# The first product of experts 1 to 7 by one level of Strassen's method, all of it ahead of the second product

## The chip, the core and the metric

The kernel runs on one core of one Trainium2 chip. The metric is the device time of one launch in microseconds (us). The core has TensorE (PE, with its weight loads PEld), VectorE (DVE), ScalarE (ACT), GpSimd (POOL) and SyncE (SP), which here only issues transfers. Matmuls accumulate into PSUM, which has 8 banks of 128 x 512 numbers in single precision; all other tiles lie in SBUF, 128 partitions wide.

## The reference, cut to what matters

Attention over q, k, v (4 batches, 8 heads, 768 positions, 64 numbers a head; a window of 128 positions and 4 sink positions) gives 3072 rows x of 512 numbers. A gate picks two of eight experts for each row, with weights that sum to one. Then:

```python
out = np.zeros((N, D), dtype=np.float32)          # N = 3072, D = 512, F = 1024, E = 8
for e in range(E):
    for k in range(2):
        mask = top2[:, k] == e
        if not mask.any():
            continue
        h = np.maximum(x[mask] @ w1[e], 0.0)          # first product, 512 -> 1024
        out[mask] += top2_w[mask, k, None] * (h @ w2[e])   # second product, 1024 -> 512
```

## The kernel before, in words

**Arithmetic.** Inputs are single precision. Each factor is split in a high and a low part, and one block product is three matmuls: high weight by high x, high by low, low by high. Here ScalarE writes the high part and VectorE (a subtraction) the low part, for weights, rows and the hidden layer; some of expert 0's low parts are POOL's.

**Order.** A class `Plan` collects operations, each with an engine, an estimated cost, a priority and the tiles that it reads and writes. `Plan.run` simulates a list scheduler with those costs and then writes every operation out in the simulated order, so each engine's order is fixed when the program is built. Tiles stand in rings of two to nine buffers; a buffer's next use waits for the last reader of its previous use. A first plan holds the attention of all batches, the routing of the first three and the start of expert 0; a second plan holds the routing of the last batch, the rest of expert 0 and experts 1 to 7.

**Experts.** Experts 1 to 7 are sorted by load at run time; a table `who` holds their numbers (the loads of weights read it from a register) and `perm` picks a row's weight. Experts 0 to 7 in this order have room for 832, 832, 832, 800, 800, 768, 768, 768 rows: six tiles of 128 rows, and for the first five a seventh, narrow tile of 64 or 32. Each of experts 1 to 7 is worked in two pieces, tiles 0 to 2 (384 rows) and the rest (448, 416 or 384); expert 0 in pieces of 512 and 320 rows, the first of rows of the first three batches.

**A piece.** For each of 8 blocks of 128 hidden columns: the first product (`up`, 4 x 3 matmuls, L1070 to L1072, into one of two banks `H`), relu into the high part (`up_h`, ACT, L1081) and the low part (`up_l`, DVE, L1088) of a hidden tile `h` (ring of nine), then the second product of that block (`down`, L1099 to L1101, three matmuls for each full tile of rows into one of four banks `Y`; a narrow tile takes two, L1104 and L1105). So groups of 12 first-product matmuls alternate with 9 or 11 of the second product. The last piece alone does all its first products first and then its second products tile by tile. After the last block a tile is scaled by its weight into `y` (ACT, L1108; for a narrow tile L1111 on ACT and L1115, L1119 on DVE) and added to the output by an indirect DMA, which POOL issues (L1123, behind a memset of `spacer`, L1122; ring of four). The output is filled with zeros ahead of it (`out<-zt`, L1268, issued on SP).

**Rows.** The rows lie in a DRAM table `x_rows`, 4 parts of 128 numbers and 8 weights each. Expert 0 gathers whole rows (L897 on POOL, one indirect DMA a tile), and its tiles are transposed on PE (`TX`, L947). Experts 1 to 7 gather in quarters of 32 rows (L903, ring `xg` of five), each pair or triple of them behind a one-element copy on POOL that waits for a certain hidden block (`gate`, L1132). VectorE picks a row's weight (`gw`, `wc`, L1036, L1038) and transposes the tile in 32 x 32 blocks (L952, `xtn`); ACT writes the high part (L961, `skn`) and DVE the low part (L197, `sqn`). L197 is the line of a helper `minus` that all subtractions go through.

**Weights.** Each expert has four chunks of W1 (all 512 rows by 256 columns) and four of W2 (256 rows by 512), 512 KB each, through a staging ring `st` of two (L998 in four transfers a chunk, L1005 in one), ACT L1008 for the high part (`w`, `w2a`, `w2b`) and DVE L197 for the low part.

**Routing of the last batch.** It ends with matmuls on PE that place each row in its expert's list ("placing", L812) and spread the lists (L859); the late rows of expert 0 are gathered behind it.

Of the kernel before, what the change touches and what calls it, by code (L numbers as in the profile page):

```python
# [46 lines left out]
class Plan:  # L47
# [5 lines left out]
    def __init__(self, nc, pools, rings, cold=0.0):  # L53
# [8 lines left out]
        self.wrote = {}  # L62

    def get(self, tag, i, shape=None, dt=F32, pool="sb", pad=None):
        kx = (tag, i)
# [4 lines left out]

    def op(self, eng, dur, prio, fn, r=(), w=(), u=(), lat=None, kind=0):
# [4 lines left out]
        for kx in list(r) + list(w) + list(u):  # L76
# [88 lines left out]

class Shape:
# [33 lines left out]
def attention(tc, plan, consts, cst, sh, q, k, v, xbuf):  # L200
# [6 lines left out]
    plan.rings.update(vr=2, kn=2, qn=2, vn=2, dv=2, skn=2, sqn=2, kq=2, C=5, mn=3, sm=4, ri=2, pc=3,  # L207
# [323 lines left out]
def routing_setup(nc, pool, tmp, cst, sh, w_gate, w_noise, noise):  # L531
# [45 lines left out]
    c["quad"] = quad[1]  # L577
    c["most"] = pool.tile([128, 1], F32, name="most")
# [63 lines left out]
def routing(nc, plan, cst, sh, b, t0, nt, z, xbuf):  # L642
# [188 lines left out]
    if ends:  # L831
# [8 lines left out]
        if last:  # L840
# [9 lines left out]
            ordered(lambda: rt("idr", [128, E - 1, TE]), "idw")  # L850
        else:
            dve(lambda: v.tensor_tensor(tab("idx"), where()[:, fl], tab("sa"), op=OP.add), [("X", xi), ("sa", i)], [("idx", i)], .13)
    if last:
# [3 lines left out]
        def spread():  # L857
            for q in range(4):
# [31 lines left out]
def gather(plan, nc, cst, sh, xbuf, e, t, z, after=None):  # L890


    n = sh.TE * e + t
    first = not e and t < sh.FA

    def go():
        nc.gpsimd.indirect_dma_start(  # L897
            out=plan.get("xg", n, [128, sh.XW], F32, "early"), out_offset=None, in_=xbuf[:128 + sh.NA] if first else xbuf,
            in_offset=bass.IndirectOffsetOnAxis(ap=cst["idg"][:, t:t + 1], axis=0))

    def part(i):
        x = plan.get("xg", n, [128, sh.XW], F32, "early").rearrange("p (i d) -> p i d", d=sh.SW)
        nc.gpsimd.indirect_dma_start(  # L903
# [485 lines left out]
```

## Time and profile before

| | |
|---|---|
| runs | 806.75, 802.84, 803.80 us; median 803.8 |
| profiled execution, span | 802.8 us |
| matmuls on PE | 4753; busy 772.3 us (96%) |
| DVE, ACT, POOL busy | 54%, 43%, 55% |
| attention and routing, start of expert 0 | 0 to about 220 us |
| expert 0 with the last batch's routing | about 220 to 305 us |
| experts 1 to 7 | 305 to 795.2 us |
| last store | 795.2 to 802.8 us |

Rows of groups read: line, engine, operation, tiles (`out<-in`), partitions by columns, count; then busy time and mean ns of one; then the idle time of the engine just before them and what ended it. Rows of the timeline read: start in us, duration, engine, line, operation. Rows of a stretch read: from:to, length, busy time of PE, PEld, DVE, ACT and POOL with the number of instructions, the granted clock of TensorE (1 is full speed), the mean busy share of the 16 DMA engines and the GB/s. Rows of waits read: who waits, for whom, then total us, count and mean. Busy times of PE overlap, since matmuls are pipelined.

### The profile page before, as it was taken

The page shows a single profiled execution, that of the slowest core. Times are in us where ns is not written, and L with a number is a line of the kernel's source. Part 1 is how long each engine was busy: PE and PEld are TensorE (multiplying, and loading weights), DVE is VectorE, ACT ScalarE, POOL GpSimd, SP SyncE. Part 2 cuts the span into 40 slices and gives each one's busy share as a digit, 9 for nine tenths or more (in the row PEclk, how much of TensorE's full clock was granted, in tenths as well). Part 3 has the DMA queues.
Part 4 walks back from the last instruction along what each step waited for, and adds up shares of the span by engine and source line. Part 5 has one row for each costly group of instructions (what it writes and reads, how often), then busy time and mean ns, then how long its engine had stood idle before and what let it go on. Part 6 is the DMA issues. An engine that isn't in the chain of part 4 may idle for free.

```text
span 802.8 us, 13806 instructions
## 1 busy us (share of the span) xinstructions
PE 772.3 (96%) x4753; PEld 656.1 (82%) x4753; DVE 434.3 (54%) x1115; ACT 342.6 (43%) x695; POOL 441.5 (55%) x669
## 2 busy tenths in 40 slices
PE   7999999899798999999999999999999999999996
PEld 4776777677577888988988898899889999999994
DVE  5888897798565345354435434542553363364320
ACT  5877778686420334244233413332442343334121
POOL 5757657778604447473745456374636647366222
PEclk9999999999999999999999999999999999999998
DMA  6769767845526196264526535561744365174133
GB/s 121 169 150 200 162 155 207 181 120 129 152 90 175 22 257 152 45 140 128 102 38 158 141 56 94 144 119 37 147 123 94 73 172 121 26 175 97 32 40 40
DMA packets 151193, 96.03 MB, mean 120 GB/s; under 512 B 100528, under 2 KB 129200, under 8 KB 151120
## 3 DMA queue, kind: packets, MB, share of 16 engines
q1 hardware_dynamic: 137744, 67.93, 32.6%
q0 software_dynamic: 13376, 27.19, 19.4%
q8 instruction: 38, 0.62, 0.3%
q14 instruction: 35, 0.29, 0.1%
HBM read 66.89 MB, written 28.20 MB: 118 GB/s over the span
## 4 chain that ended last, share of the span: by engine, by line
PE 64%; issue 4%; DMA 2%; POOL 2%; DVE 1%; SPq 0%; ACT 0%; POOLq 0%; DVEq 0%; ACTq 0%
PE H L1070 11%; PE H L1072 10%; PE H L1071 10%; PE Y L1099 10%; PE Y L1101 10%; PE Y L1100 10%; POOL out L1123 1%; PE Y L1104 1%; PE Y L1105 1%; DMA xg<-x_rows,idg 1%; DMA out<-y,idx 1%; DMA st<-in_moe_w 1%; SPq L1268 0%; PE T L947 0%; PE X L616 0%
## 5 line engine op out<-in xcount | busy, mean ns | idle before, releaser
L903 POOL DMA_INDIRECT xg<-x_rows,rt_idq x174 | 175.8, 1010 | 62.1 <-issue 51.7
L1070 PE MATMUL H<-skn,w 128*128 128x384 f32 (+4 forms) x512 | 178.3, 348 | 0.0
L1072 PE MATMUL H<-skn,w 128*128 128x384 f32 (+4 forms) x512 | 176.8, 345 | 0.0
L1071 PE MATMUL H<-sqn,w 128*128 128x384 f32 (+4 forms) x512 | 176.3, 344 | 0.0
L1088 DVE SCALAR_TENSOR_TENSOR h<-H,h 128x384 fp32r<-128x384 f32 (+4 forms) x168 | 75.5, 469 | 184.7 <-ACT h L1081 184.5
L1081 ACT ACTIVATE h<-H 128x384 fp32r<-128x384 f32 (+4 forms) x128 | 64.6, 505 | 249.4 <-PE H L1072 249.3
L1132 POOL COPY spacer<-h 1x1 f32<-1x1 f32 x88 | 26.6, 303 | 167.3 <-ACT h L1081 167.1
L1123 POOL DMA_INDIRECT out<-y,idx x53 | 89.2, 1683 | 50.4 <-ACT y L1108 34.6
L1070 PEld LDWEIGHTS H<-skn,w 128*128 128x128 f32 x512 | 96.6, 189 | 7.7 <-issue 0.8
L1071 PEld LDWEIGHTS H<-sqn,w 128*128 128x128 f32 x512 | 96.6, 189 | 6.9
L1072 PEld LDWEIGHTS H<-skn,w 128*128 128x128 f32 x512 | 96.4, 188 | 3.0
L1101 PE MATMUL Y<-w2b,h 128*128 128x512 f32 x192 | 75.2, 392 | 1.1 <-DVE h L1088 1.1
L1099 PE MATMUL Y<-w2b,h 128*128 128x512 f32 x192 | 75.5, 393 | 0.6 <-ACT h L1081 0.6
L1099 PE MATMUL Y<-w2a,h 128*128 128x512 f32 x192 | 75.5, 393 | 0.0
L1100 PE MATMUL Y<-w2b,h 128*128 128x512 f32 x192 | 75.2, 392 | 0.0
L1100 PE MATMUL Y<-w2a,h 128*128 128x512 f32 x192 | 75.1, 391 | 0.0
L1101 PE MATMUL Y<-w2a,h 128*128 128x512 f32 x192 | 74.9, 390 | 0.0
L197 POOL TENSOR_TENSOR cbuf<-cbuf,mn 128x528 f32<-128x528 f32 x48 | 52.6, 1098 | 18.5 <-DVE mn L330 10.7
L310 PE MATMUL S<-kq 64*128 64x264 f32 (+1 forms) x384 | 56.4, 410 | 1.0 <-DVE ri L348 0.5
L961 ACT ACTIVATE skn<-xtn 128x512 fp32r<-128x512 f32 (+2 forms) x46 | 27.9, 606 | 63.3 <-DVE xtn L952 63.2
L197 DVE TENSOR_TENSOR w<-st,w 128x1024 fp32r<-128x1024 f32 x28 | 34.3, 1224 | 17.8 <-ACT w L1008 17.8
L1101 PEld LDWEIGHTS Y<-w2b,h 128*128 128x128 f32 x192 | 36.1, 188 | 9.4 <-DVE h L1088 1.6
(209 smaller groups left out, 1359.6 us busy)
## 6 DMA issues: line engine op xcount, KB each, us to landing
st<-in_moe_w SPq DMA_DIRECT2D x36, 512.0 KB
st<-in_moe_w SPq DMA_DIRECT2D x112, 128.0 KB
out<-zt SPq DMA_DIRECT2D x31, 256.0 KB
vn<-in_v SPq DMA_DIRECT2D x16, 384.0 KB
x_rows<-xr SPq DMA_DIRECT2D x48, 128.0 KB
kn<-in_k SPq DMA_DIRECT2D x30, 192.0 KB
qn<-in_q SPq DMA_DIRECT2D x30, 192.0 KB
xg<-x_rows,rt_idq POOLq DMA_INDIRECT x174, 2.9
```

Source lines behind the costliest of these rows:

```text
L197: eng.tensor_tensor(out, a, b, op=OP.subtract)
L310: nc.tensor.matmul(p[:, :2 if j else 1], kq(g)[r, j // 2, 2 + j % 2, NS:], x[:, :2 if j else 1], start=True, stop=True)
L903: nc.gpsimd.indirect_dma_start(out=x[:, i, :], out_offset=None, in_=xbuf.rearrange("r (q d) -> (r q) d", d=sh.SW), in_offset=bass.Indirect ...
L1070: nc.tensor.matmul(p, w[:, 0, i], xh, start=(i == 0), stop=False)
L1071: nc.tensor.matmul(p, w[:, 0, i], xl, start=False, stop=False)
L1072: nc.tensor.matmul(p, w[:, 1, i], xh, start=False, stop=(i == DC - 1))
L1081: nc.scalar.activation(get("h", FC * q + f, [128, 2 * 128 * FIRST], F32R)[:, :width], get("H", FC * q + f), AF.Relu)
L1088: nc.vector.scalar_tensor_tensor(h[:, o:o + s1 - s0], p[:, s0:s1], 0.0, h[:, s0:s1].bitcast(F32), op0=OP.max, op1=OP.subtract)
L1099: nc.tensor.matmul(p, hh, w[:, 0], start=(f == 0), stop=False)
L1100: nc.tensor.matmul(p, hh, w[:, 1], start=False, stop=False)
L1101: nc.tensor.matmul(p, hl, w[:, 0], start=False, stop=(f == FC - 1))
L1123: d = nc.gpsimd.indirect_dma_start(out=out, out_offset=bass.IndirectOffsetOnAxis(ap=c["idx"][:size(e, t), e, t:t + 1], axis=0), in_=get("y ...
```

## The change

Experts 1 to 7 do the first product by one level of Strassen's method in Winograd's form. W1 is halved in rows and in columns, and the expert's rows are halved (tiles 0, 1, 2 and half of the narrow tile against tiles 3, 4, 5 and the other half), so that x.W1 is a 2 x 2 block product. It takes 7 products of half size in place of 8: for each of 4 groups of 128 + 128 hidden columns 7 products of 6 matmuls over 416, 400 or 384 columns, 168 matmuls an expert in place of 192 (8 blocks of two pieces of 12); 1176 in place of 1344 for the seven experts. Three of the products take plain blocks of W1, four take sums of blocks; three take plain halves of x, four take sums. New work:

- POOL makes the four sums of each W1 chunk in place in `st` (L1083 one addition, L222 three subtractions, 128 x 256 each); ACT and DVE split the plain blocks and the sums (2 + 1 operations each).
- DVE transposes a pair of tiles into a raw tile `rw` (L1329), splits it, mixes its quarters (four subtractions), splits the result, into a fixed tile `XO`.
- Three banks a group: ACT copies three partial results to `ts` (L1394), DVE adds three others to them (`total`, L1400), then relu (ACT L1411) and the low part (DVE L1418), into one fixed hidden tile `hid` for all 8 blocks.
- All 28 products of an expert stand ahead of its second products (L1274 to L1276, narrow tile L1278 and L1279), whose tiles end staggered by up to two blocks (`SKEW`); tiles keep one bank for all 8 blocks. Expert 0 does its 8 first products ahead of its second ones too, in each piece.
- All 8 banks are fixed and shared by name (`B`, `H`, `Y`, `X`, `TX`); weights stand in one fixed tile `Z` with three slots for mixed W1 chunks (`W`, `Wd`) and three for W2 chunks (`V`); `xg` has four buffers, `st` two, `y` four.
- The gates are gone; gathers are issued up to four tiles ahead. Expert 1 gathers whole rows (seven DMAs with `idg1`), transposes on PE and loads each W1 chunk in one transfer; experts 2 to 7 keep the quarters. The planner counts 1.05 us for a quarter gather where it counted 1.25, 1.7 for a store as before, 0.72 for a sum on POOL.
- The zero fills hang on the blocks of expert 0's first piece, no longer on both pieces.

The diff, cut to its core (`mixed_x` and the aliases of the fixed buffers are told above):

```diff
 def gather(...):
-    for i in range(min(128, sh.CAPS[e] - 128 * t) // 32):
-        plan.op("Pool", 1.25, z + i, lambda i=i: part(i), r=[("rt_idq", sh.B - 1)] + (after(t, i) if after else []),
-                w=[("xg", n, i)], u=[("xg", n)], lat=3)
+    if e < 2:
+        plan.op("Pool", 1.25, z, row, r=[("idg1", 0) if e else ("idg", int(not early))], w=[("xg", n)], lat=3)
+        return n
+    for i in range(size // 32):
+        plan.op("Pool", 1.05, z + i, lambda i=i: part(i), r=[("idq", 0)], w=[("xg", n, i)], u=[("xg", n)], lat=3)
...
+def w_mixed(plan, nc, cst, sh, w1, e, i, z):
...
+    def mix(j):
+        _, a, b, c, d = raw()
+        if j == 0:
+            nc.gpsimd.tensor_tensor(d, c, d, op=OP.add)
+        else:
+            minus(nc.gpsimd, *((c, a, c), (a, d, a), (b, b, a))[j - 1])
...
+    plan.op("ACT", .6, z, lambda: direct_hi(0, 4), st, [kd])
+    plan.op("ACT", .37, z, lambda: direct_hi(4, 2), st, [kd])
+    plan.op("DVE", .69, z + .1, lambda: direct_lo(0, 4), st, [kd])
+    plan.op("DVE", .43, z + .1, lambda: direct_lo(4, 2), st, [kd])
+    for j in range(4):
+        plan.op("Pool", .72, z + .1, lambda j=j: mix(j), [], st)
+    plan.op("ACT", 1.04, z, mixed_hi, st, [kc])
+    plan.op("DVE", 1.22, z + .1, mixed_lo, st, [kc])
...
-    def up(q, f):
-        for i in range(DC):
-            xh, xl = (x[:, i, :width] for x in both)
-            nc.tensor.matmul(p, w[:, 0, i], xh, start=(i == 0), stop=False)
-            nc.tensor.matmul(p, w[:, 0, i], xl, start=False, stop=False)
-            nc.tensor.matmul(p, w[:, 1, i], xh, start=False, stop=(i == DC - 1))
...
+    MUL = {1: ("A11", 0, 0), 5: ("S1", 6, 1), 6: ("S2", 12, 0), 2: ("A12", 2, 2), 3: ("S4", 4, 1), 7: ("S3", 10, 0), 4: ("A22", 8, 0)}
...
+        def product(f, x):
+            u, o, b = MUL[x]
+            key = ("B", B[f][b])
+            fresh = x in (1, 5, 2)
...
+                for i in range(2):
+                    wh, wl = (mixed_block(c, k, u, y, i) for y in range(2))
+                    xh, xl = (XO()[:, y, o + i, :W] for y in range(2))
+                    nc.tensor.matmul(p, wh, xh, start=(fresh and i == 0), stop=False, skip_group_check=True)
+                    nc.tensor.matmul(p, wh, xl, start=False, stop=False, skip_group_check=True)
+                    nc.tensor.matmul(p, wl, xh, start=False, stop=(i == 1), skip_group_check=True)
...
+            seq += [(f, 1), (f, 5)] + ([(f - 1, 4)] if f else []) + [(f, 6), (f, 2), (f, 3), (f, 7)]
...
+    for e in range(1, E):
+        mixed_x(e, D[e - 1] + 1 if e > 1 else -80)
...
+                mix_w(e, i, D[e - 1] + 8 + 5 * i if e > 1 else 40 + 7 * i)
...
+        load_v(e, 0, U[e] - 3)
+        def rest(e=e):
+            mix_w(e, 3, U[e] + 6)
+            load_v(e, 1, U[e] + 12)
+            load_v(e, 2, U[e] + 18)
+        ups(e, U[e], ks[e], rest)
```

The order that this makes is shown at three places; numbers behind names are those of buffers. PE first, inside expert 1 before the change: `H` banks take first products, `Y` banks second ones.

```order
L1070 MATMUL H<-skn,w_5075 128x448
L1071 MATMUL H<-sqn,w_5075 128x448
L1072 MATMUL H<-skn,w_5075 128x448
L1099 MATMUL Y<-w2b,h 128x512
L1100 MATMUL Y<-w2b,h 128x512
L1101 MATMUL Y<-w2b,h 128x512
L1104 MATMUL Y<-w2b,h 128x512
L1105 MATMUL Y<-w2b,h 128x512
```

PE after the change, where expert 1's first products end and its second ones begin (`bank` is one of the eight banks):

```order
L1384 MATMUL bank_3594<-XO,Z 128x416
L1385 MATMUL bank_3594<-XO,Z 128x416
L1386 MATMUL bank_3594<-XO,Z 128x416
L1274 MATMUL bank_3597<-Z,hid 128x512
L1275 MATMUL bank_3597<-Z,hid 128x512
L1276 MATMUL bank_3597<-Z,hid 128x512
L1384 MATMUL bank_3591<-XO,Z 128x416
L1385 MATMUL bank_3591<-XO,Z 128x416
L1386 MATMUL bank_3591<-XO,Z 128x416
L1278 MATMUL bank_3590<-Z,hid 128x512
L1279 MATMUL bank_3590<-Z,hid 128x512
```

The two kinds of product alternated through the whole expert; now they mix at this seam alone, with the first second-product groups between the last two products. In the start of the second plan, PE now has 138 matmuls of expert 0 ahead of the placing matmuls where it had 108, and 21 between these and the transposes of expert 0's late rows in both.

POOL before, during a middle expert: quarter gathers in twos and threes behind gates, and stores of finished tiles between them.

```order
L903 DMA xg<-x_rows,rt_idq 128x136 x2
L1132 COPY spacer<-h 1x1
L903 DMA xg<-x_rows,rt_idq 128x136 x3
L1132 COPY spacer<-h 1x1
L903 DMA xg<-x_rows,rt_idq 128x136 x2
L1132 COPY spacer<-h 1x1
L903 DMA xg<-x_rows,rt_idq 128x136 x2
L1122 MEMSET spacer 1x1
L1123 DMA out<-y,idx 3968x512
```

POOL after, as the next expert's first chunk of W1 has been staged:

```order
L941 DMA xg_77<-x_rows,idqt 128x136
L1083 TENSOR_TENSOR st_72<-st_72 128x2x128
L941 DMA xg_74<-x_rows,idqt 128x136
L222 TENSOR_TENSOR st_72<-st_72 128x2x128
L941 DMA xg_74<-x_rows,idqt 128x136
L222 TENSOR_TENSOR st_72<-st_72 128x2x128
L941 DMA xg_74<-x_rows,idqt 128x136
L222 TENSOR_TENSOR st_72<-st_72 128x2x128
```

The gates left the queue, and the sums of W1 came in between the gathers of the next expert's rows.

DVE before, inside expert 1: low parts of hidden blocks (L1088) with weights and rows of the next piece between them.

```order
L1088 SCALAR_TENSOR_TENSOR h<-H,h 128x384
L1088 SCALAR_TENSOR_TENSOR h<-H,h 128x64
L197 TENSOR_TENSOR w_4910<-st,w_4910 128x1024
L1036 TENSOR_TENSOR gw<-xg,perm 32x8 x4
L1038 TENSOR_REDUCE wc_126<-gw 128x1
L952 STREAM_TRANSPOSE xtn<-xg 128x512
L1088 SCALAR_TENSOR_TENSOR h<-H,h 128x384
```

DVE after, near the end of expert 1's first products:

```order
L1400 TENSOR_TENSOR ts<-ts,bank_3597 128x416
L1400 TENSOR_TENSOR ts<-ts,bank_3594 128x416
L1329 STREAM_TRANSPOSE rw<-xg_75 128x4x4x32
L1418 SCALAR_TENSOR_TENSOR hid<-ts,hid 128x384
L1418 SCALAR_TENSOR_TENSOR hid<-ts,hid 128x32
L968 TENSOR_TENSOR gw_3602<-xg_75,permq 128x32
L970 TENSOR_REDUCE wc_138<-gw_3602 128x1
L1418 SCALAR_TENSOR_TENSOR hid<-bank_3597,hid 128x384
```

The totals (`ts`) and the hidden low parts stand in one queue with the transposes and weight rows (`gw`) of the next expert's gathered tiles.

More of the change, by code (lines that the diff above doesn't have):

```diff
@@ L887, in experts_setup, with gather, row @@
     c["wc"] = [pool.tile([128, sh.TE], F32, name=f"wc{i}") for i in range(2)]
[L890 to L896, printed above, removed]
+def gather(plan, nc, c, sh, xbuf, e, t, z):
+    n = plan.next("xg")
+    size = min(128, sh.CAPS[e] - 128 * t)
+    early = not e and t < sh.FA
+    def row():
+        idx = c["idg1"] if e else c["idg"]
         nc.gpsimd.indirect_dma_start(
-            out=plan.get("xg", n, [128, sh.XW], F32, "early"), out_offset=None, in_=xbuf[:128 + sh.NA] if first else xbuf,
-            in_offset=bass.IndirectOffsetOnAxis(ap=cst["idg"][:, t:t + 1], axis=0))
+            out=plan.get("xg", n, [128, sh.XW], F32, "early")[:size], out_offset=None, in_=xbuf[:128 + sh.NA] if early else xbuf,
+            in_offset=bass.IndirectOffsetOnAxis(ap=idx[:size, t:t + 1], axis=0))
@@ L1099, in down, with products @@
+    def products(p, f, w, hh, hl, both, r):
+        if both is None:
             nc.tensor.matmul(p, hh, w[:, 0], start=(f == 0), stop=False)
@@ new lines, in products, with XO, temp, raw @@
+            nc.tensor.matmul(p[:2 * r], both, w[:, 0], start=(f == 0), stop=False)
+            nc.tensor.matmul(p[:2 * r], both, w[:, 1], start=False, stop=(f == FC - 1))
+    def XO():
+        return get("XO", 0, [128, 2, 14, sh.CAP // 2], F32R, "late")
+    def temp(n):
+        return get("ts", 0, [128, 4, sh.CAP // 2], F32, "late")[:, n % 4]
+    def raw(n):
+        return get("rw", 0, [128, 2, 8, 128], F32, "late")[:, n % 2]
+    def pairs(e):
+        return [(0, 3), (1, 4), (2, 5)] + ([(TF,)] if R[e] else [])
@@ new lines, in experts, with alias @@
+    sh_xg = {e: {} for e in range(E)}
+    for t in range(FA, TE):
+        n = gather(plan, nc, c, sh, xbuf, 0, t, -110)
+        weight(plan, nc, c, sh, 0, t, n, -100)
+        rows_turn(plan, nc, c, sh, t, size(0, t), "TX", -100, n)
+    U, D = {}, {}
+    U[0], D[0] = 0.0, first(0, 0.0)
+    at = first(1, D[0])
+    for e in range(1, E):
+        U[e], D[e] = at, at + 168 * cost(sh.CAPS[e] // 2)
+        at = D[e] + FC * sum(.69 if t < TF else .46 for t in tiles_of(e))
+    def alias(k, *keys):
+        plan.behind[k] = keys
```

682 lines of the change are left out of this document (449 added, 233 removed).

## The prediction

> **What bounds the kernel now.** First the page's engine totals, then a split of the span at the places where the work changes character, then the waits of TensorE alone.
>
> ```profile
> span 802.8 us, 13806 instructions
> PE 772.3 (96%) x4753; PEld 656.1 (82%) x4753; DVE 434.3 (54%) x1115; ACT 342.6 (43%) x695; POOL 441.5 (55%) x669
> ...
> 0.00:220.00 220.00, 201.68 (x1902) 149.43 (x1902) 178.76 (x484) 155.53 (x401) 149.94 (x290) 0.99 0.68 159
> 220.00:305.00 85.00, 80.42 (x434) 65.96 (x431) 43.51 (x136) 23.74 (x40) 29.47 (x44) 0.98 0.50 135
> 305.00:795.20 490.20, 490.20 (x2423) 440.71 (x2421) 212.07 (x495) 162.66 (x253) 260.48 (x336) 1.00 0.46 101
> 795.20:802.80 7.60, 0.01 (x1) 0.00 (x0) 0.00 (x0) 0.69 (x1) 1.57 (x1) 0.66 0.29 36
> ...
> PE TX L947 <- DMA xg<-x_rows,idg: 2.7, 1, 2.7
> PE Y L1101 <- DVE h L1088: 1.1, 1, 1.1
> PE Y L1099 <- ACT h L1081: 0.6, 1, 0.6
> ```
>
> The stretches list length, then busy time of PE, PEld, DVE, ACT and POOL. From 305 to 795.2 us, experts 1 to 7, TensorE is busy 490.20 of 490.20 us, while DVE is at 43%, ACT at 33% and POOL at 53%. After 220 us TensorE waits three times, 4.4 us in all. So a microsecond of matmul taken out of that stretch is a microsecond of the end, as long as the three other engines, which have room, stay in time. The attention up to 220 us keeps its order; the tail of 7.6 us (last store) keeps its form. Both are costed at nothing.
>
> **The matmuls removed.** Busy times of matmuls overlap, so I price by the distance of starts. The first and the thirteenth start of groups of twelve, and of nine matmuls of the second product:
>
> ```profile
> 308.49 0.34 PE L1070 MATMUL H<-skn,w 128*128 128x384 f32 x1
> 310.60 0.40 PE L1099 MATMUL Y<-w2a,h 128*128 128x512 f32 x1
> ...
> 347.04 0.37 PE L1070 MATMUL H<-skn,w 128*128 128x448 f32 x1
> 349.49 0.39 PE L1099 MATMUL Y<-w2a,h 128*128 128x512 f32 x1
> ...
> 506.76 0.35 PE L1070 MATMUL H<-skn,w 128*128 128x416 f32 x1
> 509.04 0.39 PE L1099 MATMUL Y<-w2b,h 128*128 128x512 f32 x1
> ...
> 641.26 0.40 PE L1099 MATMUL Y<-w2a,h 128*128 128x512 f32 x1
> 643.32 0.34 PE L1070 MATMUL H<-skn,w 128*128 128x384 f32 x1
> ```
>
> Twelve take 2.11 us at 384 columns, 2.28 at 416, 2.45 at 448. Before, one expert has eight rounds of both pieces: 8 x (2.11 + 2.45) = 36.5 us for 832 rows, 8 x (2.11 + 2.28) = 35.1 for 800, 8 x 4.22 = 33.8 for 768; for two, two and three experts 244.5 us. After, each has 28 products of 6 matmuls over half the rows: 168 x 0.190 = 31.9 us (416 columns), 168 x 0.183 = 30.7 (400, midway between rows), 168 x 0.176 = 29.6 (384); together 214.0. **Term 1: -30.5 us.** The second product keeps its matmuls, 8 x 20 x 0.229 (2.06 us for nine) = 36.6 us for 832 or 800 rows, 33.0 for 768. Per expert TensorE then needs 68.5 us (832), 67.3 (800) and 62.6 (768).
>
> **Alternation.** Nine second-product matmuls between two first-product groups take 2.06 us. If the pairing costs 0.03 us each of 16 x 7 times, its removal gives 3 us; if nothing, 0. The new order still alternates near the seam. **Term 2: -2 us** (0 to -3).
>
> **Transposes of expert 1.** They move from VectorE's 32-blocks to TensorE, seven tiles; the row of such a tile and the start after it:
>
> ```profile
> 263.00 0.60 PE L947 MATMUL TX<-idf,xg 128*128 128x128 f32 x4
> 263.35 0.47 PE L1099 MATMUL Y<-w2b,h 128*128 128x512 f32 x1
> ```
>
> 7 x 0.35: **term 3: +2.5 us.** Expert 1's 26 quarter gathers become 7 row gathers on POOL, and its four weight loads issue once each instead of four times on SP: both are relief. The zero fills moved up in SP's queue, ahead of the loads of the experts' numbers, lie beside expert 0's 44 us of matmuls; if that cover failed, expert 1's first weights would be late by those issues, a delay that the bounds of term 4 hold.
>
> **The start.** Expert 0 now runs all eight first products before its second. Ahead of the placing matmuls of the last routing stand 138 of its matmuls instead of 108, so the routing ends 30 x 0.229 = 6.9 us later; between the placing and the first transposes stand 21 in both, so the 2.7 us wait for the gather stays. Behind the routing VectorE has some 25 us of rows (durations below) before expert 1's first product, TensorE some 41 us of expert 0: covered. Cost nothing; if the wait went, -2.7; if the late routing came through, +6.9.
>
> **The new side work.** Durations, from the rows by shape in the experts' stretch (and POOL's from the attention):
>
> ```profile
> L1088 DVE SCALAR_TENSOR_TENSOR h<-H,h 128x384 fp32r<-128x384 f32 x112 | 62.0, 553 | 170.7 <-ACT h L1081 170.4
> L197 DVE TENSOR_TENSOR w<-st,w 128x1024 fp32r<-128x1024 f32 x27 | 33.1, 1224 | 17.4 <-ACT w L1008 17.4
> L952 DVE STREAM_TRANSPOSE xtn<-xg 128x512 f32<-128x512 f32 x40 | 28.1, 702 | 0.0
> L197 DVE TENSOR_TENSOR sqn<-xtn,skn 128x512 fp32r<-128x512 f32 x40 | 27.5, 687 | 13.3 <-ACT skn L961 13.2
> L197 DVE TENSOR_TENSOR sqn<-xtn,skn 128x256 fp32r<-128x256 f32 x2 | 0.8, 425 | 0.1
> L1081 ACT ACTIVATE h<-H 128x384 fp32r<-128x384 f32 x80 | 39.3, 492 | 156.0 <-PE H L1072 156.0
> L1008 ACT ACTIVATE w<-st 128x1024 fp32r<-128x1024 f32 x26 | 27.4, 1055 | 13.8 <-DMA st<-in_moe_w 13.8
> ...
> L197 POOL TENSOR_TENSOR w2a<-st,w2a 128x256 fp32r<-128x256 f32 x8 | 5.7, 730 | 7.2 <-ACT w2a L1008 7.2
> ...
> 399.70 0.95 POOL L903 DMA_INDIRECT xg<-x_rows,rt_idq  x1 [0.31 <-issue]
> 400.95 0.95 POOL L903 DMA_INDIRECT xg<-x_rows,rt_idq  x1 [0.30 <-issue]
> ...
> 417.00 1.63 POOL L1123 DMA_INDIRECT out<-y,idx  x1 [0.22 <-issue]
> 418.93 1.60 POOL L1123 DMA_INDIRECT out<-y,idx  x1 [0.27 <-issue]
> ```
>
> VectorE for an 832-row expert: per pair of tiles two transposes (1.40), two weights (0.64), low parts 0.69 + 0.43 + 1.22, four mixes of 256 columns (1.70), so 6.1; three pairs 18.2, the narrow tile about 2.7; four mixed chunks 4 x (0.69 + 0.43 + 1.22) = 9.4; four second-weight chunks 4.9; twelve totals at about 0.58, 7.0; sixteen hidden low parts at about 0.55 and narrow remainders, 11.0; last store 1.2: 54 of 68 us, 80%. ScalarE by the same count with 0.49 to 1.06 us rows: about 40 of 68. Neither is the bound by its sum. In one second-product phase (37 us) VectorE has about 31 us; the mixed inputs come first in its order, about 24 us of it, so some 10 us are left before the next first product needs them. In the first-product phase a copy or total has about two products, 2.1 us, before its bank is written again.
>
> POOL is tighter: 26 gathers at 1.25 (399.70 to 400.95), 7 scatters at 1.93 (417.00 to 418.93), 16 mixes of 256 columns at 0.73: 32.5 + 13.5 + 11.7 = **58 of 68 us**; 53 of 62 for a 768-row expert. The order was set with 1.05 and 1.7 us for gather and scatter: per expert POOL falls behind that order by 26 x 0.20 + 7 x 0.23 = 6.8 us, against some 10 us free. What is late next: VectorE's weight rows `gw` wait for the gathered rows, and totals and hidden parts stand behind them; their 2.1 us of room covers the first part of a delay. So the bounds of new TensorE waits are 0 (POOL's free time takes all) and 6.8 x 7 = 48 us (none). I take about 2 us per expert, nearer to the sum that fits than to the one that doesn't: **term 4: +14 us** (0 to 48).
>
> POOL and VectorE also hold each other up:
>
> ```profile
> 307.67 1.23 DVE L197 TENSOR_TENSOR w<-st,w 128x1024 fp32r<-128x1024 f32 x1 [2.92 <-ACT w L1008]
> 308.15 0.79 POOL L1132 COPY spacer<-h 1x1 f32<-1x1 f32 x1 [0.20 <-ACT h L1081]
> ...
> 190.74 0.73 POOL L197 TENSOR_TENSOR w<-st,w 128x256 fp32r<-128x256 f32 x1
> 190.87 1.28 DVE L197 TENSOR_TENSOR dv<-vn 128x640 f32<-128x640 f32 x1
> ```
>
> A copy of one element lasts 0.79 us and ends with VectorE's two-input operation (308.90); a VectorE subtraction of 640 columns begun behind a POOL operation lasts 1.28 us, where the 512- and 1024-column rows (687 and 1224 ns) give 0.82. In the new kernel most of VectorE's rows have two inputs in SBUF and POOL has 16 mixes per expert. If each mix meets one and costs the other up to 0.73 us, VectorE rises by at most 11.7 to 66 of 68 us: that still fits, and is inside term 4. The Trainium skill (SBUF — State Buffer, "Who interferes with whom") says that only the pair of ports of these two engines contends, as an exclusive lock. By that rule the port's own time, VectorE's two-input work of some 46 us and 12 us of mixes, would be 58 of 68, and by it alone term 4 would be near 0; these two pairs of rows agree with the lock.
>
> **The sum.** 802.8 - 30.5 - 2 + 2.5 + 14 = 786.8 us. The profiled span is about 1.0 below the median of 803.8, so the forecast for the median is **788 us**.
>
> **Rivals.** *All covered:* term 4 is 0; 773 + 1 = **774** (771 to 780). For it: every sum above fits, and gathers run up to four tiles ahead. Against it: three engines at 58 to 85% in fixed orders, each waiting for the others.
>
> *POOL sets the pace* (the other side): all of its lag reaches TensorE through `gw`: 774 + 48 = **822**. It decides from 4.3 us per expert upward, since 30 us of gain in seven experts is that much. Against it: POOL's sum is below TensorE's.
>
> *The clock falls at every seam.* What one wait did in this trace:
>
> ```profile
> 254.70:257.46 2.76, 0.01 (x2) 0.00 (x1) 0.80 (x3) 0.00 (x0) 1.77 (x2) 1.00 0.99 362
> 257.46:261.83 4.37, 4.37 (x15) 3.50 (x15) 1.22 (x5) 0.60 (x1) 1.09 (x2) 0.61 0.56 216
> 261.83:266.20 4.37, 4.37 (x24) 3.36 (x23) 1.29 (x2) 1.18 (x3) 1.46 (x3) 1.00 0.00 0
> ```
>
> After 2.76 us without work the granted clock was 0.61 for 4.37 us, a loss of 4.37 x 0.39 = 1.7 us. One such wait per expert costs 7 x (2.76 + 1.7) = 31 us: 774 + 31 = **805**, no change. The Trainium skill (TensorE: Matmul & The Clock Gate, "HAM oscillation — how this bites in real kernels") warns of just such recurring gaps; it puts the threshold at about 3.4 us, and here 2.76 us was enough. Against it: since 305 us this trace has no wait, and a wait split over several products stays short.
>
> *The saving isn't there:* if a group of six cost as much as seven of a twelve, nothing would be won. The rows speak against it: the cost per matmul follows the columns and each matmul has a weight load already (4753 of both).
>
> **Chances.** Forecast (781 to 799.8) 0.50; all covered 0.27; no change (799.8 to 807.8) 0.11, of it the clock 0.06, the saving that isn't there 0.02, other waits 0.03; slower 0.12, of it POOL 0.09. A change within 0.5%, 4 us, is about what a measurement of this kernel can't tell from none. So faster 0.77, same 0.11, slower 0.12. The range that leaves out at most 2 in 10 goes from 772 into the eaten case: 772 to 806.
>
> **What would show it.** After the change the first product's matmuls should number 1176 for experts 1 to 7 and start 0.176 to 0.190 us apart inside a group; TensorE's idle time after 305 us should be near 14 us, with VectorE totals (`ts`), `gw` or stored tiles as releasers; VectorE should be near 75% and POOL near 85% busy in that stretch, mixes near 0.73 us. Wrong would be: waits above 30 us; mixes or gathers that grow past 1.2 and 1.6 us under the port; the start of expert 1 late by 10 us because its mixed inputs wait for the routing.

## The result, and the profile after

The changed kernel takes 835.3 us (834.25 to 837.70, four runs) beside 803.6 for the kernel before; the ratio is 1.039 (95% interval 1.036 to 1.041). The forecast was 788, faster. Medians here and below leave out runs over 1.5% above the fastest of their kernel. First the stretch of experts 1 to 7 of the kernel before (304.56 to 795.05), then the page's totals and the same stretch after (308.55 to 824.78), each from the first matmul of expert 1 to the end of the last matmul; columns as in the prediction.

```profile
304.56:795.05 490.49, 490.49 (x2425) 441.15 (x2423) 212.26 (x497) 162.66 (x253) 260.92 (x336) 1.00 0.46 101
```

```profile
span 836.1 us, 13853 instructions
PE 768.6 (92%) x4613; PEld 639.2 (76%) x4613; DVE 571.7 (68%) x1284; ACT 426.3 (51%) x903; POOL 518.9 (62%) x674
...
308.55:824.78 516.23, 482.04 (x2249) 420.85 (x2247) 342.52 (x639) 240.03 (x444) 327.18 (x341) 0.97 0.43 96
```

TensorE had no idle time in the stretch before; now 516.2 - 482.0 = 34.2 us are idle, and the granted clock is 0.97 in place of 1.00. Yet VectorE is busy for 66%, ScalarE for 46% and POOL for 63% of the stretch: no engine is full. The 33.3 us between the two profiled executions are made up as follows. The matmuls need some 31 us less (490.5 to the forecast's 459.4, the sum of its per-expert needs; a run below comes to 467 with hardly a wait). The stretch is 516.2 - 459.4 = 57 us longer than that need: 34.2 us of waits, 482.0 - 464.6 = 17.4 us in which the same matmuls ran slower than in that later run, and 464.6 - 459.4 = 5.2 us that the forecast priced them too low. Expert 1 starts 4.0 us later, and from the last matmul to the end of the program it is 11.3 us where it was 7.75.

What TensorE waits for and what stands behind that on ScalarE; then POOL's own long waits in the stretch; then POOL's instructions and two of VectorE's (305 to 780 us, grouped by shape):

```profile
PE bank L1384 <- ACT ts L1394: 21.6, 13, 4.7
PE bank L1384 <- ACT Z L1088: 5.6, 3, 2.7
...
ACT Z L1088 <- POOL st L222: 51.5, 15, 7.5
ACT y L1179 <- DMA out<-y,idx: 19.5, 13, 4.2
```

```profile
POOL xg L941 <- DVE rw L1329: 78.2, 7, 19.0
...
POOL st L1083 <- DVE Z L222: 34.9, 5, 19.3
POOL out L1194 <- ACT y L1179: 32.4, 9, 13.5
```

```profile
L941 POOL DMA_INDIRECT xg<-x_rows,idqt x139 | 155.4, 1118 | 109.8 <-DVE rw L1329 78.2 <-issue 28.4 <-DVE ts L1400 0.6
L222 POOL TENSOR_TENSOR st<-st 128x256 f32<-128x256 f32 x78 | 74.6, 957 | 1.6
L1194 POOL DMA_INDIRECT out<-y,idx x43 | 73.7, 1713 | 11.9 <-issue 6.0 <-ACT y L1179 3.6 <-ACT hid L1411 0.9
L1083 POOL TENSOR_TENSOR st<-st 128x256 f32<-128x256 f32 x26 | 27.4, 1054 | 23.0 <-DVE Z L222 22.8
L222 DVE TENSOR_TENSOR XO<-rw,XO 128x1024 fp32r<-128x1024 f32 x18 | 25.8, 1434 | 2.2 <-ACT XO L1335 2.1
L1193 POOL MEMSET spacer<- 1x1 f32 x43 | 23.1, 538 | 0.0
L1418 DVE SCALAR_TENSOR_TENSOR hid<-ts,hid 128x16 fp32r<-128x16 f32 x24 | 8.0, 334 | 0.0
```

Sums last 0.96 to 1.05 us where 0.73 was counted. These durations overlap: a memset and often a sum are recorded as begun while the instruction before still runs. In the stretch POOL's work, its busy time and the short gaps between its instructions together, is 327.2 + 41 = 368 us, where the planner's costs for its 136 gathers, 48 stores and 108 sums give 302. Yet POOL itself stands for 78.2 + 34.9 + 32.4 = 145.5 us at the head of its queue, waiting for the other engines. One seam, where expert 1's second products end and expert 2's first ones begin, ScalarE, POOL and TensorE in order of time; then the clock in pieces of 4 us:

```profile
390.99 1.06 ACT L1129 ACTIVATE Z<-st 128x1024 fp32r<-128x1024 f32 x1 [1.67 <-DMA st<-in_moe_w]
391.47 2.40 POOL L1083 TENSOR_TENSOR st<-st 128x256 f32<-128x256 f32 x1
392.13 1.74 POOL L1193 MEMSET spacer<- 1x1 f32 x1
393.50 0.69 ACT L1179 ACTIVATE y<-bank,wc 128x512 f32<-128x512 f32 x1 [1.45 <-DMA out<-y,idx]
394.08 0.51 ACT L1394 ACTIVATE ts<-bank 128x416 f32<-128x416 f32 x1
394.64 0.71 PE L1384 MATMUL bank<-XO,Z 128*128 128x416 f32 x1 [3.95 <-ACT ts L1394]
```

```profile
392.00:396.00 4.00, 1.36 (x4) 1.31 (x5) 1.23 (x1) 1.24 (x4) 3.80 (x6) 0.60 0.92 147
396.00:400.00 4.00, 4.00 (x14) 3.82 (x13) 0.72 (x2) 2.30 (x5) 3.61 (x6) 0.54 0.81 156
400.00:404.00 4.00, 4.00 (x23) 3.95 (x22) 3.93 (x10) 3.93 (x8) 3.54 (x6) 1.00 0.70 97
```

The bank that the copy to `ts` reads is done at 389.57, but the copy starts at 394.08: it stands on ScalarE behind a weight split that waits for its chunk until 390.99, and behind the scaling of a finished tile, which waits 1.45 us for a `y` buffer. The store that frees this buffer was issued at 388.40, 1.8 us after its tile was scaled, behind two gathers on POOL. TensorE waits 3.95 us, and the granted clock is 0.50 from 392.82 to 399.65. In the whole stretch it is at 0.50 for 29.7 us, in seven pieces, and for 25.4 of them TensorE is at work: this costs some 13 us of the 17.4.

So the seam is not the stores alone. Over all 21.6 us of TensorE's waits for `ts`, ScalarE was idle for a `y` buffer for 4.4 us, for sums for 2.2 and for a weight chunk for 0.8; most of the rest it was working off what stood ahead of the copy.

### The profile page after: what moved, and what is told of

It reads as the page before. It is cut to its first block, busy times and chain, and to the rows that moved or that the text cites. A ratio compares the mean times of both kernels' runs of the same rounds, so it can differ in the third digit from the quotient of the medians.

```text
span 836.1 us, 13853 instructions
## 1 busy us (share of the span) xinstructions
PE 768.6 (92%) x4613; PEld 639.2 (76%) x4613; DVE 571.7 (68%) x1284; ACT 426.3 (51%) x903; POOL 518.9 (62%) x674
## 4 chain that ended last, share of the span: by engine, by line
PE 28%; POOL 17%; DVE 10%; DMA 9%; issue 5%; ACT 4%; SPq 0%; POOLq 0%; DVEq 0%; ACTq 0%
POOL xg L941 8%; POOL st L222 5%; PE bank L1276 4%; PE bank L1274 4%; PE bank L1275 4%; DVE Z L222 4%; DMA st<-in_moe_w 4%; DMA out<-y,idx 3%; PE bank L1384 3%; PE bank L1386 3%; PE bank L1385 3%; DMA xg<-x_rows,idqt 2%; POOL out L1194 2%; POOL st L1083 2%; PE bank L1226 2%
## 5 line engine op out<-in xcount | busy, mean ns | idle before, releaser
L941 POOL DMA_INDIRECT xg<-x_rows,idqt x148 | 170.3, 1151 | 111.9 <-DVE rw L1329 78.2
L1384 PE MATMUL bank<-XO,Z 128*128 128x384 f32 (+2 forms) x392 | 142.3, 363 | 30.1 <-ACT ts L1394 21.6
L222 DVE TENSOR_TENSOR Z<-st,Z 128x1024 fp32r<-128x1024 f32 (+2 forms) x114 | 105.1, 929 | 76.6 <-ACT Z L1088 47.0
L1276 PE MATMUL bank<-Z,hid 128*128 128x512 f32 x384 | 152.1, 396 | 1.6 <-DVE hid L1236 1.6
L1274 PE MATMUL bank<-Z,hid 128*128 128x512 f32 x384 | 152.4, 397 | 0.0
L1275 PE MATMUL bank<-Z,hid 128*128 128x512 f32 x384 | 151.9, 396 | 0.0
L1386 PE MATMUL bank<-XO,Z 128*128 128x384 f32 (+2 forms) x392 | 139.5, 356 | 2.9 <-DVE Z L222 2.9
L1385 PE MATMUL bank<-XO,Z 128*128 128x384 f32 (+2 forms) x392 | 139.3, 355 | 0.0
L1194 POOL DMA_INDIRECT out<-y,idx x53 | 89.6, 1690 | 45.7 <-ACT y L1179 32.4
L1384 PEld LDWEIGHTS bank<-XO,Z 128*128 128x128 f32 x392 | 77.2, 197 | 39.9 <-ACT ts L1394 26.4
L1276 PEld LDWEIGHTS bank<-Z,hid 128*128 128x128 f32 x384 | 72.2, 188 | 19.5 <-DVE hid L1236 2.0
L1274 PEld LDWEIGHTS bank<-Z,hid 128*128 128x128 f32 x384 | 72.0, 188 | 17.0 <-ACT hid L1231 0.5
L1275 PEld LDWEIGHTS bank<-Z,hid 128*128 128x128 f32 x384 | 72.1, 188 | 15.8
L222 POOL TENSOR_TENSOR st<-st 128x256 f32<-128x256 f32 x84 | 80.1, 954 | 1.9
L1386 PEld LDWEIGHTS bank<-XO,Z 128*128 128x128 f32 x392 | 77.2, 197 | 5.0 <-DVE Z L222 4.5
L1385 PEld LDWEIGHTS bank<-XO,Z 128*128 128x128 f32 x392 | 77.4, 197 | 1.8
L1400 DVE TENSOR_TENSOR ts<-ts,bank 128x384 f32<-128x384 f32 (+2 forms) x84 | 46.9, 563 | 37.2 <-PE bank L1386 36.1
L1418 DVE SCALAR_TENSOR_TENSOR hid<-ts,hid 128x384 fp32r<-128x384 f32 (+2 forms) x132 | 62.3, 508 | 6.7 <-ACT hid L1411 6.6
L1411 ACT ACTIVATE hid<-ts 128x384 fp32r<-128x384 f32 (+4 forms) x116 | 46.9, 436 | 35.5 <-DVE ts L1400 35.2
L1088 ACT ACTIVATE Z<-st 128x1024 fp32r<-128x1024 f32 x28 | 29.6, 1058 | 67.1 <-POOL st L222 60.0
L222 POOL TENSOR_TENSOR cbuf<-cbuf,mn 128x528 f32<-128x528 f32 x48 | 52.6, 1097 | 18.0 <-DVE mn L355 10.5
```

Source lines behind the costliest of these rows:

```text
L222: eng.tensor_tensor(out, a, b, op=OP.subtract)
L941: nc.gpsimd.indirect_dma_start(out=x[:, i, :], out_offset=None, in_=xbuf.rearrange("r (q d) -> (r q) d", d=sh.SW), in_offset=bass.Indirect ...
L1194: d = nc.gpsimd.indirect_dma_start(out=out, out_offset=bass.IndirectOffsetOnAxis(ap=c["idx"][:size(e, t), e, t:t + 1], axis=0), in_=get("y ...
L1274: nc.tensor.matmul(p, hh, w[:, 0], start=(f == 0), stop=False)
L1275: nc.tensor.matmul(p, hh, w[:, 1], start=False, stop=False)
L1276: nc.tensor.matmul(p, hl, w[:, 0], start=False, stop=(f == FC - 1))
```

## The experiments

Kernels sent together ran on one chip, beside the kernel before (802.7 to 804.8 in every group). There were five groups, and the changed kernel's first measurement; the end of this section says why the groups can't simply be compared.

**Group 1: which theory.** Theory 1 was the stores (four `y` buffers for seven tiles that end together), theory 2 POOL's sums.

```diff
-y=4, ... rw=1, raw=2            # y6
+y=6, ... rw=1, raw=1
-SKEW = 2                        # skew4
+SKEW = 4
-            nc.gpsimd.tensor_tensor(d, c, d, op=OP.add)      # mixdve, and the three subtractions with it
+            nc.vector.tensor_tensor(d, c, d, op=OP.add)
-        plan.op("Pool", .72, z + .1, lambda j=j: mix(j), [], st)
+        plan.op("DVE", .43, z + .1, lambda j=j: mix(j), [], st)
```

In prod8 the 7 products of a group, of 6 matmuls each, become 4 plain ones of 12, with no sums, mixes, copies and totals; VectorE's work in the stretch falls with them from 342.5 to 187.2 us. y6 has six `y` buffers at the price of one raw tile in place of two.

> Two more buffers for finished tiles (six y in place of four; the room comes from keeping one raw tile rw in place of two). Theory 1 (stores): at the end of an expert seven tiles finish within some 8 us, and a y buffer is taken for about 9 us (scaling 0.7, store issued behind others about 2.2, landing 6.4), so ACT's fifth store waits some 4 us and the copies to ts behind it hold PE up, 21.6 us in all, and the clock falls after it, some 16 us: with six buffers the waits for out<-y fall from 19.5 to under 6 us, PE's waits for ts copies from 21.6 to under 8, and the time to 798 to 812. Theory 2 (POOL's sums of W1 and their contention with VectorE hold PE up through late weights): PE's waits only change place, 825 to 838.

> SKEW 4 in place of 2, all else as in the changed kernel: the seven tiles of an expert end over four blocks (about 18 us) in place of two. Theory 1: four buffers then last four times 2.6 = 10 us, longer than the 9 us that one is taken, so waits for out<-y go below 6 us and PE's waits for ts copies below 8; against it the fourth W2 chunk has less time in its three slots, so some of the gain is lost to waits of second products on Z: 800 to 818. Theory 2: no gain, 828 to 840.

> The four sums of each W1 chunk on VectorE in place of POOL (16 an expert, 0.43 us each there). Theory 1: the stores' round trip of 9 us with four buffers stays, PE's waits for ts copies stay above 12 us: 820 to 838. Theory 2: POOL is free of 106 us of sums and its stores and gathers come sooner; PE's waits fall below 12 us in all and the time to 795 to 810.

> The order and the buffers of the changed kernel (all first products of an expert ahead of its second ones, four y, seven tiles ending together), but eight plain products in place of seven mixed ones: no sums of W1, no mixes of x, no copies and totals, 192 matmuls an expert in place of 168, all outputs computed. Theory 1 (the order's stores are the cause): PE needs 490 us of matmuls and the waits at the seams stay, since banks come free with the stores: 820 to 845. Theory 2 (the mixing work is the cause): near the kernel before, 800 to 808.

| | us | ratio to before (interval) |
|---|---|---|
| y6 | 835.5 | 1.041 (1.035 to 1.047) |
| skew4 | 833.2 | 1.035 (1.029 to 1.041) |
| mixdve | 808.4 | 1.005 (1.002 to 1.009) |
| prod8 | 811.6 | 1.008 (1.006 to 1.011) |

TensorE's and ScalarE's waits with six buffers, and with SKEW 4:

```profile
ACT y L1179 <- DMA out<-y,idx: 10.9, 3, 5.0
PE bank L1384 <- ACT ts L1394: 18.1, 13, 3.9
...
PE bank L1384 <- ACT XO L1335: 6.8, 3, 5.6
```

```profile
PE bank L1384 <- ACT ts L1394: 22.8, 7, 5.3
ACT y L1179 <- DMA out<-y,idx: 21.4, 6, 4.6
```

Neither settles theory 1. Six buffers took 8.6 us from ScalarE's waits for stores and 3.5 from TensorE's for `ts`, but with one raw tile TensorE waited 6.8 us for `XO`; SKEW 4 left the waits for stores as they were. prod8 says more: it has the same order, the same four buffers and the same seven tiles at a seam, ScalarE waits longer for stores than in the changed kernel, and TensorE does not wait at all in its stretch:

```profile
ACT y L1173 <- DMA out<-y,idx: 31.2, 15, 4.1
...
306.30:799.60 493.30, 493.30 (x2417) 441.77 (x2415) 187.18 (x373) 157.77 (x264) 215.84 (x228) 1.00 0.44 98
```

So "all first products ahead" by itself costs nothing there (493.3 against 490.5 us); its 8 us are the later start (306.3), the longer end (11.3) and the 2.8. So the stores alone do not hold TensorE; it takes the mixing work, all of which prod8 leaves out. (Its time lies above the 800 to 808 expected of theory 2.) With the sums on VectorE TensorE's waits for `ts` fell from 21.6 to 6.2 us, but a new one came:

```profile
PE bank L1226 <- DVE hid L1236: 11.4, 2, 8.8
PE bank L1384 <- ACT ts L1394: 6.2, 4, 2.5
```

Before the longer of these two waits, 8.8 us at the end of expert 0, VectorE stood idle for 3.93 and 4.40 us for gathered rows, whose transposes were ahead of expert 0's hidden low parts in its queue; expert 1's sums were done by then. Theory 2 named the right work, and its 795 to 810 held the time; that TensorE's waits would fall below 12 us in all did not hold (11.4 + 6.2).

**Group 2: work or order.** honest changes three numbers of the planner; tiny lets each sum work on 4 of 256 columns, so W1 is mostly left unmixed; d1 takes the sums to VectorE for experts 2 to 7 alone, with honest's gather and store costs; d1y6 adds y6's buffers.

```diff
-        plan.op("Pool", 1.05, z + i, lambda i=i: part(i), ...      # honest
+        plan.op("Pool", 1.26, z + i, lambda i=i: part(i), ...
-        op("Pool", 1.7, z, scatter, ...
+        op("Pool", 2.2, z, scatter, ...
-        plan.op("Pool", .72, z + .1, lambda j=j: mix(j), [], st)
+        plan.op("Pool", 1.0, z + .1, lambda j=j: mix(j), [], st)
-        _, a, b, c, d = raw()                                       # tiny
+        _, a, b, c, d = (x[:, :, :2] for x in raw())
+    eng, own, us = (nc.gpsimd, "Pool", 1.0) if e == 1 else (nc.vector, "DVE", .43)   # d1
```

> The changed kernel with the planner's costs near those of its trace: quarter gather 1.26 (was 1.05), store 2.2 (was 1.7), sum of W1 on POOL 1.0 (was 0.72); the same work on the same engines in another order. Theory A (order): the fixed order of ACT stands on sums that POOL delivers later than planned, the high parts of mixed weights (L1088) wait 51.5 us at the head of ACT's queue and stores and ts copies wait behind them; with true costs they move back, and the time falls to 803 to 820. Theory B (work): POOL's sums and VectorE's two-input work lengthen each other (sums 0.73 to 0.96, VectorE by some 54 us in all), and no order of the same work helps: 826 to 840.

> The order of the changed kernel word for word, but each sum of W1 on POOL works on 4 of its 256 columns, so that the weights are mostly left unmixed: the instructions, their queue and their waits stay, their work goes. Theories A and B both give 793 to 810, as the sums then take some 0.1 to 0.3 us; if the time stays above 822, neither the sums' length nor their port is the cause, but the queue of gathers and stores.

> Sums of W1 on VectorE for experts 2 to 7 and on POOL for expert 1 alone, with the planner's true costs of gathers and stores. When all sums were VectorE's the time was 809 and 11.4 us of TensorE's waits were for expert 0's hidden low parts, behind expert 1's sums: these go, with the clock that falls after them. Theory A and B: 790 to 801, faster than the kernel before. If VectorE is simply full (70% busy), 803 to 812.

> As d1, with six y buffers and one raw tile. The stores' wait for a buffer was 13.2 us on ACT with all sums on VectorE and 6.2 us of TensorE's waits were for ts copies behind it; with six buffers these fall below 3 us: 4 to 8 us below d1, 785 to 797. If the stores are no part of it, within 2 us of d1.

honest 814.0 (ratio 1.015, 1.010 to 1.020); tiny 791.1 (0.986, 0.982 to 0.990); d1 784.6 (0.977, 0.974 to 0.980); d1y6 795.2 (0.990, 0.987 to 0.994). Their stretches, in this order without d1y6; behind honest's, ScalarE's wait for sums, TensorE's longest waits and POOL's sums; ahead of tiny's, ScalarE's wait for sums:

```profile
302.93:796.72 493.79, 474.64 (x2249) 412.10 (x2247) 346.30 (x637) 238.53 (x443) 318.35 (x342) 0.99 0.45 101
```

```profile
ACT Z L1088 <- POOL st L222: 7.8, 6, 2.0
...
PE bank L1386 <- DVE Z L222: 6.4, 8, 1.5
...
PE bank L1384 <- ACT Z L1088: 5.0, 2, 3.3
...
L222 POOL TENSOR_TENSOR st<-st 128x256 f32<-128x256 f32 x80 | 83.0, 1040 | 1.4
```

```profile
ACT Z L1088 <- POOL st L222: 26.5, 11, 5.4
...
305.30:777.50 472.20, 465.49 (x2249) 411.21 (x2247) 300.34 (x638) 239.69 (x443) 259.23 (x341) 1.00 0.47 105
```

```profile
303.74:771.18 467.44, 464.60 (x2249) 411.54 (x2247) 339.62 (x734) 238.91 (x443) 237.70 (x245) 1.00 0.46 106
```

The changed kernel was not in this group; it is compared by its first measurement, whose trace, like all of this group's, shows none of the late starts told of below. Theory A (order) is borne out for about half: the same work on the same engines, sums as long as before (1.04 us), but planned with truer costs, is 21 us faster, and TensorE's waits for `ts` fall from 21.6 to 0.8 us. What honest still waits for is mostly the mixed weights themselves, low parts above all. Taking the sums' work away, with the order word for word, gives 44 us. Theory B's "no order helps" fell; whether another order would mend the rest was not tried. ScalarE's own wait for sums is no measure of the loss: tiny keeps 26.5 us of it, while TensorE's waits for `ts` are down to 5.5. d1 bears out the forecast's arithmetic of matmuls: 467.4 us with 2.8 us of waits, against 459.4. tiny and d1 came out 2 and 5 us below their expected ranges. Six buffers with one raw tile made it slower by 10 us, not faster by 4 to 8: its trace shows 2.2 us of new waits for `XO` and 4.6 for `ts`, which is not all of the 10.

**Group 3: what of d1 is what.** d1old is d1 with the planner's old gather and store costs, d1s3 is d1 with SKEW 3, raw1 is y6 with four `y`.

> Sums on VectorE for experts 2 to 7, on POOL for expert 1, with the planner's old costs of gather (1.05) and store (1.7): tells what of the 24 us between all sums on VectorE (809) and d1 (785) is expert 1's and what the costs'. If expert 1's sums on VectorE (the 11.4 us wait at expert 0 and the clock behind it) are the cause: 785 to 792. If the costs of gathers and stores are: 800 to 810.

> As d1 with SKEW 3: the tiles of an expert end over three blocks. d1 has some 4 us of TensorE's waits left, 2.8 of them for ts: at best 781 to 785; if the third slot of W2 chunks comes too late, 786 to 795.

> The changed kernel with one raw tile rw in place of two and the four y buffers as they are: the other half of the run with six y buffers. If one raw tile costs nothing, 833 to 838 and six y buffers gave nothing; if it is 840 or more, six y buffers gave the difference to 835.

844.7 (ratio 1.048, 1.040 to 1.057), 829.3 (1.033, 1.025 to 1.042), 839.1 (1.041, 1.033 to 1.049): d1's two neighbours lie 45 to 60 us above it, far outside what was expected of them. But the traces of this group show ScalarE and VectorE idle for up to 12 us at a time with nothing behind it that the profile can name. So d1 was measured again beside them.

**Groups 4 and 5.**

> d1 once more, beside the runs it is to be compared with. Its first time, 784.6, was taken in another group than those of d1old (844.7) and d1s3 (829.3), and the traces of that last group show ACT and VectorE idle for 5 to 12 us with nothing behind it that a trace of the other groups shows (waits named remote and issue). If that belongs to the group: about 785 here. If d1's own time was a lucky one: 800 or more.

> d1old once more beside d1: 785 to 792 if expert 1's sums on VectorE were what held the run with all sums there (809); 800 to 812 if the planner's costs of gathers and stores were; 835 or more if the order is so touchy that its costs alone bring 50 us.

> d1 with SKEW 3 once more beside d1: 781 to 795 if the last group was disturbed, 820 or more if SKEW 3 is what costs it.

> The changed kernel itself in the same group as the three above, as their reference: 833 to 838.

> d1 a third time: 784.6 in a group whose traces show no idle time without a releaser, 814.2 in a group whose traces do. 783 to 788 where the trace shows none, 800 to 816 where it does.

> The changed kernel's order with sums of 4 columns on POOL, again: 789 to 796 if the group is undisturbed. If it is disturbed and d1 loses 30 us in it, about 800 to 820, since the stalls then meet any order of this work.

> All sums of W1 on VectorE, expert 1's too, with the planner's costs of gathers at 1.26 and stores at 2.2: the fourth of four combinations (all on VectorE with the old costs 809; expert 1's on POOL with the old costs 840 to 845, with the true costs 785 to 814). If true costs of POOL's queue are what helps, 785 to 800; if expert 1's sums on VectorE hold expert 0 up as before, 803 to 815.

| | first | group 4 | group 5 |
|---|---|---|---|
| the changed kernel | 835.3 | 840.9 | |
| d1 | 784.6 (group 2) | 814.2 | 816.2 |
| d1old | 844.7 (group 3) | 839.5 | |
| d1s3 | 829.3 (group 3) | 829.3 (two runs) | |
| tiny | 791.1 (group 2) | | 825.4 |
| dh | | | 833.5 |

In dh all sums are VectorE's, with honest's gather and store costs; neither of its expected ranges held it, and the changed kernel (833 to 838) and tiny (800 to 820) missed theirs too. In group 4 d1 is 27 us below the changed kernel, where it was 51 in the undisturbed groups, and above the kernel before (ratio 1.012, 1.007 to 1.016; 1.014, 1.011 to 1.017 in group 5). So d1 beats the kernel before on one chip of three, and can't be called a better kernel. Inside group 4, d1old and the changed kernel differ by 1.4 us: there, moving the sums of experts 2 to 7 to VectorE gives nothing measurable without the truer costs of gathers and stores, and 27 us with them. And in group 5 tiny, without the sums' work, lies above d1. So that work and order are the cause is shown for undisturbed runs alone. One place where d1's two traces part shows how its 30 us are lost. Group 4's, at the end of expert 4's first products, ScalarE, VectorE and POOL; then the same two instructions of ScalarE in group 2's:

```profile
546.34 0.51 ACT L1413 ACTIVATE hid<-bank 128x400 fp32r<-128x400 f32 x1 [3.35 <-PE bank L1388]
...
550.40 0.94 POOL L941 DMA_INDIRECT xg<-x_rows,idqt  x1 [0.30 <-issue]
551.65 0.95 POOL L941 DMA_INDIRECT xg<-x_rows,idqt  x1 [0.30 <-issue]
552.07 0.50 ACT L1396 ACTIVATE ts<-bank 128x400 f32<-128x400 f32 x1 [4.71 <-remote]
554.93 0.57 DVE L1402 TENSOR_TENSOR ts<-ts,bank 128x400 f32<-128x400 f32 x1 [6.83 <-remote]
```

```profile
534.62 0.50 ACT L1413 ACTIVATE hid<-bank 128x400 fp32r<-128x400 f32 x1
...
535.64 0.51 ACT L1396 ACTIVATE ts<-bank 128x400 f32<-128x400 f32 x1
```

TensorE issues the same matmuls in both, 8.26 us apart, up to 546.4; the bank that L1413 reads is done at the same place in both. Less those 8.26 us, ScalarE takes it up 3.5 us later in group 4; the copy behind it then waits 4.7 us more and is 8.2 us later; and VectorE resumes 2.3 us after the end of the last of a row of gathers that POOL issues back to back (2.4 after the end of that copy). The table counts ScalarE's, VectorE's and TensorE's waits of over 1 us without a nameable releaser that end between 310 and 790 us, and how many of them end within, or up to 3 us behind, four or more quarter gathers with no other instruction of POOL between them:

| | waits without releaser | of these at a row of gathers |
|---|---|---|
| first measurement, honest, tiny, d1, d1y6, mixdve, skew4 | none | |
| y6, prod8 | 1 (2.5 us), 2 (6.8 us) | 1, 1 |
| group 3: d1old, d1s3, raw1 | 22 (67.5), 31 (91.3), 16 (37.3) | 21, 31, 16 |
| group 4: d1, d1old, d1s3, changed | 14 (42.8), 19 (61.4), 23 (71.1), 19 (52.4) | 14, 19, 23, 13 |
| group 5: d1, tiny, dh | 11 (41.7), 26 (71.6), 23 (66.5) | 11, 12, 23 |

Such rows, with 3 us behind each, fill 36 to 45% of the stretch in these runs (22 to 24% in tiny and the changed kernel, where sums stand between many gathers), so nearly all waits at rows is far more than chance; half of tiny's and a third of the changed kernel's lie elsewhere. The rows (up to 16 gathers) are in every one of these kernels, in the undisturbed groups too. What differs between the groups is not shown by any trace; the kernel before, whose gates break its gathers up into twos and threes, seldom four, keeps its time in all of them.

## Why the prediction was wrong

- **Term 1 held but for some 5 us.** The changed trace counts 3 x 392 = 1176 first-product matmuls, inside a group 0.176 to 0.190 us apart, and d1's stretch of 467.4 us is 8 us over the forecast's 459.4, 2.8 of them waits: the matmuls were priced some 5 us too low.
- **Term 2 was nothing.** prod8 does all first products ahead and its stretch is 2.8 us longer, not shorter: pairing the two products cost nothing measurable. 2 us of the error.
- **Term 3** was 2.5 and the start came 4.0 later; the end of the program, costed at nothing, took 3.6 more. No run says why. The end is the same in all kernels of this form read for it (11.3 in the changed kernel, prod8 and d1); the start is not (302.9 in honest, 303.7 in d1, 308.6 here), so it hangs on order and work too.
- **Term 4 is the step that failed**: +14, bounds 0 to 48; measured 57 by the stretch, or 52 without the 5 us that belong to the price of the matmuls. TensorE's waits alone, 34.2 us, lie inside the bounds, but above the 30 that the prediction itself called wrong. It failed in three places. The path first: the forecast let POOL's lag reach TensorE through `gw` on VectorE. It came through ScalarE, which was called not the bound by its sum and left there: 21.6 + 5.6 of the 34.2 us wait for ScalarE's `ts` copies and mixed weights. In a fixed order a half idle engine still stops at its head. The high parts of mixed weights waited 51.5 us for sums there, with scalings and `ts` copies behind them; with truer costs (honest) that wait is 7.8 us and the time 21 us less. Then the cover: "POOL's free time takes all" was the lower bound, and POOL was late and idle by turns. By its work above it fell behind the planner by 66 us, 9.8 for each of the 6.75 experts whose sums lie in the stretch, where 6.8 was forecast and some 10 said to be free; but 145.5 us of its free time lay where it waited itself, and there it helped nobody. Thirdly the bounds: they held waits alone. The clock was a rival of its own at 805, one wait of 2.76 us and its half clock per expert. The trace has six waits above 2 us, about one per expert, and the half clock costs some 13 us on top of them. The two came together, and the forecast had priced them as alternatives.
- **The rival "POOL sets the pace", 822 with 0.09,** named the right engine, but not its path, and POOL was busy for only 63% of the stretch (85% forecast), VectorE for 66% (75%). Busy shares said that all would fit. In undisturbed runs d1 shows that it can: with the sums of six experts on VectorE the stretch is 8 us over the need. The same engines with truer costs (honest) are 34 us over it, where the changed kernel is 57.
- **The ports.** The forecast put the mutual delay inside term 4 at up to 11.7 us of VectorE's time. A sum on POOL went from 0.73 to 0.98; a sum of 4 columns still took 0.45 us in tiny, so much of a sum's time does not go by its columns; and VectorE's rows grew: the 1024-column split takes 1434 ns, the 16-column hidden part 334, where with the sums on VectorE (mixdve) they take

```profile
L222 DVE TENSOR_TENSOR XO<-rw,XO 128x1024 fp32r<-128x1024 f32 x18 | 21.8, 1213 | 0.0
L1418 DVE SCALAR_TENSOR_TENSOR hid<-ts,hid 128x16 fp32r<-128x16 f32 x24 | 4.1, 170 | 0.0
```

The Trainium skill (SBUF — State Buffer, "Who interferes with whom") calls this pair of ports an exclusive lock, and by its sum alone term 4 would have been near 0. The rows agree with a lock, and so does a pair inside the changed trace: the same 16-column row takes 162 ns where one of its two inputs is a PSUM bank. The sum was the wrong question, since what counts is when a fixed order has what it waits for.

What stays open: how the 44 us of the sums' work split between their length, the lock and the lateness that they cause; whether some order of the same work loses less than honest's; and what the later groups' chips do at rows of gathers.

## What to carry to other kernels

When a change adds work to engines with room, and the order of every engine is fixed ahead, don't sum busy times: list what each engine's queue holds behind the first instruction that will be late, on the half idle engines too, and price the planner's costs by distances of starts in the kernel that will run, since durations that overlap count double. A wait of TensorE cost its own length and, for most waits of 2.3 us and more here, 1.7 to 2.5 us lost at half clock behind it; both belong in the bounds. And compare variants of one kernel within one group of runs: here the same program moved by 30 us between groups while its reference stood still.

## What the runs showed of the hardware that was not expected

The clock fell after a wait of 2.30 us (at 621 us; the clock of the next 10 us was 0.83) and after a pair of 1.42 and 0.61 us (at 342 us; 0.50 from 345.04 to 348.45), while one of 2.35 us at 767 us and a pair of 1.44 and 0.62 at 426 us left it at 1.00. The Trainium skill (TensorE: Matmul & The Clock Gate, "HAM oscillation — how this bites in real kernels") puts the threshold at about 3.4 us. The measured waits go below it, so here the length of one wait alone does not decide.

In three of five groups engines stood idle for 1 to 12 us at a time with no releaser that the profile can name, most often while POOL issued indirect gathers back to back or up to 3 us behind them; in the others the same programs (d1, tiny, the changed kernel) showed none of it. Its cause is not shown. That the kernel before breaks its gathers up by gates, and keeps its time in all groups, fits with the rows of gathers being part of it, but no run put the gates back.
